# Clearing the padding rows of the first chunk with VectorE and ScalarE, and a reordered prologue, in a fused Fourier-mixing and SwiGLU kernel

## The chip, the cores and the metric

The kernel runs on one core of one Trainium2 chip. The core has a matrix engine (TensorE, PE in the profile; its weight loads are PEld), VectorE (DVE), ScalarE (ACT), GpSimd (POOL) and SyncE (SP), and 16 DMA engines that move data for all of them. The metric is the device time of one launch in microseconds. Before the change it was 624.73 us, the median of five runs (624.17 to 628.4).

## What is computed

The input `x` is 8 x 3008 x 256 (batches, rows, columns) in float32. The kernel takes the real part of the two-dimensional Fourier transform of each batch (over rows and columns) and feeds it, as 24064 tokens of 256 values, to a SwiGLU block with a hidden width of 1536:

```python
def _attn_ref(x):
    X = np.fft.fft(x, axis=1)
    X = np.fft.fft(X, axis=2)
    return X.real.astype(np.float32)

def _moe_ref(x, w_gate, w_val, w_out):
    g = x @ w_gate
    silu = g * (1.0 / (1.0 + np.exp(-g)))
    val = x @ w_val
    return (silu * val @ w_out).astype(np.float32)
```

## The kernel before

**The arithmetic.** The transform over the 256 columns is folded into the weights: `w_gate` and `w_val` are multiplied once by cosine and sine tables (`CD`, `SDt`), which gives `Wp`, `Wq` and `Wm` (`Wq` times -2, 0 for the first row). The transform over the 3008 rows is a product with cosine and sine tables `Tab`, after the eight-fold symmetry of the rows has been used up by sums and differences ("folding"). Each batch is therefore held as two chunks of SBUF partitions: chunk A (`XA`, 128 rows of each eighth) and chunk C (`XC`, the remaining `NCR` = 60 rows). In chunk C 64 partitions belong to each half, of which 60 hold rows of the input, one holds row 0, and the rest is padding that has to be zero.

**The main part.** The results of the row transform, `Pt` and `Qt`, are cut into tiles of 512 (the first ones 480) columns. For each tile and each of the 12 slices of the hidden width, TensorE makes the gate and the value (line 904), ScalarE takes SiLU, VectorE and GpSimd make the products `hp` and `hm`, and TensorE multiplies them with `Wo` (line 1144). GpSimd folds the next batches at the same time (lines 157 to 181), SyncE loads them. The order of all instructions of this part comes from a small planner in the file (`Sched.run`), whose costs and due times don't depend on the prologue.

**The prologue.** Batch 0 takes another way, written out by hand in the order of issue of each engine:

- SP and ACT load chunk A of batch 0 (lines 247 and 249, five transfers) and chunk C of batch 0 into a tile of its own, `XC0` (line 260: `what` 2 are the two 240 KB transfers of the rows that run upwards, `what` 0 and 1 the four of 120 KB that run downwards), and row 0 into partitions 60 and 124 (line 261).
- The padding of `XC0` and later that of `XC` is cleared by DMA from a zero row of `sel` (`zeros`, lines 251 and 264, two transfers each). Line 261 writes partitions that line 251 clears, so it waits for these. Then SP issues the loads of batch 1 into `XC` (lines 140 to 144).
- VectorE makes the phase factors `mM` from `pcol`, GpSimd the products `t1` (line 332), VectorE the angles `rr` and `ra` (336, 340), ScalarE the tables `Tab` (343, 346).
- `place` (line 413) puts the rows in order by a product with the 0/1 matrices `putA` and `putC`: `psA` from `XA`, `psC` from the first half of `XC0` (its upward rows). `sums` (422) adds or subtracts the downward rows. `fold_d` (480, 481) folds chunk A on GpSimd and casts on ScalarE to `EOb`; `halves` (426, 427) casts chunk C to `SBc`.
- TensorE then runs `half_folded` (468) on `EOb`, `half_w` (447) on the first third of the weights, `W0` in the code and `W` in the profile, and `unfolded` (475) on `SBc`. ScalarE takes the weights `Wq` (449) and `od` (612) from PSUM, VectorE adds and subtracts to `Pt` and `Qt` (617), and the main part starts.
- The weights are loaded by GpSimd with a cast to bf16 (`load_w`, line 360): `W0` first, the second third after `fold_d`, and the last third after the first `half_w`.

GpSimd also makes `prod` = `df` times `pcol` or `pcol2` (390), from it the angles `rrd` of the column tables (391, 392, 394), and `putC` (395). `d_tables` (402 to 405) makes `CD` and `SDt` on ScalarE.

Every transfer issued by SP or ACT carries one of eight completion counters in turn. The compiled instruction list makes a queue wait, before it issues a transfer, until the last transfer with the same counter has landed. `zero` is a column of zeros, `P` is 128 and `D` is 256.

Of the kernel before, what the change touches and what calls it, by code (L numbers as in the profile page):

```python
# [12 lines left out]
F32 = mybir.dt.float32  # L13
I32 = mybir.dt.int32
BF16 = mybir.dt.bfloat16
AF = mybir.ActivationFunctionType
Alu = mybir.AluOpType
# [14 lines left out]
def kernel(  # L32
# [84 lines left out]
    def rows_at(b, row, ap):  # L117
        return bass.AP(tensor=x.tensor, offset=(b * M + row) * D, ap=ap)
# [118 lines left out]
    nc.vector.memset(zero, 0.0)  # L237
    nc.vector.memset(sel, 0.0)
    nc.scalar.activation(w0[:, 0, 0:1], zero, AF.Silu)
    zrow = sel.bitcast(F32)[1:2, :]  # L240

    def zeros(X, hi):
        dst = X.rearrange("p a q d -> p (a q d)")[64 * hi + NCR:64 * hi + 64, :]
        return dict(out=dst.rearrange("p (k n) -> p k n", n=P // 2),
                    in_=zrow.unsqueeze(1).to_broadcast([1, (64 - NCR) * dst.shape[1] * 2 // P, P // 2]))

    q.dma_start(out=XA3[:, 0:4, :], in_=up_block(0, 1, P))
    for a, eng in ((3, nc.scalar), (2, q), (1, nc.scalar), (0, q)):
        eng.dma_start(out=XA3[:, 4 + a, :], in_=down_set(0, a, JA, LA, NA))
    for hi in range(2):  # L250
        q.dma_start(**zeros(XC0, hi))

# [6 lines left out]
    for hi, what in ((0, 2), (1, 2), (0, 0), (1, 0), (0, 1), (1, 1)):  # L259
        (q, nc.scalar)[hi if what != 1 else 0].dma_start(**xc0(hi, what))  # L260
    q.dma_start(out=XC0[NCR:64 + NCR + 1:64, 0:2, 1],
                in_=rows_at(0, 0, [[2 * R * D, 2], [R * D, 2], [1, D]]))
    for hi in range(2):
        q.dma_start(**zeros(XC, hi))

# [26 lines left out]
    def col(name, n=1, dt=F32):  # L292
        small[name] = tp.tile([P, n], dt, name=name)
        return small[name]
# [13 lines left out]
    m_cols(0, pcol, LA, JA)  # L308
    vts(mM[:, 0:2], mm_[:, 0:2], scalar1=1.0 / M, scalar2=None, op0=Alu.mult)
    half = col("half")  # L310
    vts(half, pcol, scalar1=64.0, scalar2=-64.0, op0=Alu.is_ge, op1=Alu.mult)
# [7 lines left out]
    nc.vector.memset(halfpi, math.pi / 2.0)  # L319
    vts(putA, putA, scalar1=pcol, scalar2=None, op0=Alu.is_equal)  # L320
    nc.vector.memset(EOf[:, 1, :, P:P + 1], 0.0)
# [54 lines left out]
    def ce_angles(ch):  # L376
        rr, ra = ce_angle[ch]
        angles(rr, kf, ch, ti[ch])
        magnitude(ra, rr)

    def ce_tables(ch):
        rr, ra = ce_angle[ch]
        sine(ch, 0, NCE, rr)
        cosine(ch, 0, NCE, ra)

    ce_angles(0)
    nc.vector.memset(Tab[:, :, :, :, NOO - 1:NOO], 0.0)
    ce_tables(0)
    for i, c_ in enumerate((pcol, pcol2)):
        pts(prod[:, i, :], df, scalar1=c_, scalar2=1.0, op0=Alu.mult, op1=Alu.mult)  # L390
    pts(rad.bitcast(I32), prod, scalar1=1.0 / D, scalar2=1.0, op0=Alu.mult, op1=Alu.mult)
    pts(rrd, rad.bitcast(I32), scalar1=-float(D), scalar2=1.0, op0=Alu.mult, op1=Alu.mult)
    load_w(0)
    ptt(rrd, rrd, prod, op=Alu.add)
    pts(putC, putC, scalar1=pcol, scalar2=1.0, op0=Alu.is_equal, op1=Alu.mult)
    ce_angles(1)
    ce_tables(1)
    nc.vector.memset(sel[0:1, :], 1.0)
# [114 lines left out]
    opposite(0)  # L513
    d_tables()
    for a in (0, 2):
        fold_d(0, a)
    sums(SA, 1, XA, psA)
    start_acc(0)
    half_folded(0, 0)
    psC = place(XC0, putC, 2, ((psO, "o"),))  # L520
    half_folded(0, 2)
    weigh_ce()
    opposite(1)
    for a in (0, 2):
# [5 lines left out]
    for a in (0, 2):  # L530
        half_folded(1, a)
    nc.vector.memset(SDt[:, :, 0:1], 1.0)
    hd = tp.tile([P, 2, 2, 1], F32, name="hd")
# [3 lines left out]
    heads(nc.gpsimd, SC[:, 0, 0, :, 0:1], SC[:, 0, 1, :, 0:1], CEc)  # L537
    sums(SC, 1, XC0, psC)
    halves(SBc, SC, 1)
    for k, (pool, nm) in enumerate(((psV, "v"), (psG, "g"))):  # L540
# [982 lines left out]
```

## Time and profile before

| what | value |
|---|---|
| median of five runs | 624.73 us |
| the profiled execution | 624.73 us, its span 623.0 us (1.73 us lie around the span) |
| granted TensorE clock, mean | 0.993 |
| busy, PE / DVE / ACT / POOL | 604.3 / 577.0 / 527.6 / 471.8 us |
| first matmul of the main part (line 904) | 30.53 us after the span's start |
| first matmul of `psC` (line 413 on `XC0`) | 19.24 us |
| first `half_w` matmul (line 447) | 25.36 us |

Starts are given from the span's start. The profile's chain of work is followed back from the last instruction: at each step it names what released that step. A wait "A <- B: total, times, longest" says that engine and line A stood idle until B. In the timeline a row has the start, the duration, the engine and line, and the tiles; rows of one line are merged. A share of DMA time above 1 means that packets of several queues overlap on an engine.

### The profile page before, as it was taken

The page shows a single profiled execution, that of the slowest core. Times are in us where ns is not written, and L with a number is a line of the kernel's source. Part 1 is how long each engine was busy: PE and PEld are TensorE (multiplying, and loading weights), DVE is VectorE, ACT ScalarE, POOL GpSimd, SP SyncE. Part 2 cuts the span into 40 slices and gives each one's busy share as a digit, 9 for nine tenths or more (in the row PEclk, how much of TensorE's full clock was granted, in tenths as well). Part 3 has the DMA queues.
Part 4 walks back from the last instruction along what each step waited for, and adds up shares of the span by engine and source line. Part 5 has one row for each costly group of instructions (what it writes and reads, how often), then busy time and mean ns, then how long its engine had stood idle before and what let it go on. Part 6 is the DMA issues. An engine that isn't in the chain of part 4 may idle for free.

```text
span 623.0 us, 12518 instructions
## 1 busy us (share of the span) xinstructions
PE 604.3 (97%) x4012; PEld 395.4 (63%) x4073; DVE 577.0 (93%) x1054; ACT 527.6 (85%) x1001; POOL 471.8 (76%) x432
## 2 busy tenths in 40 slices
PE   7799989999999999999999999999999999999997
PEld 5445656666666666666666666666666666666676
DVE  7399959999999999999999999999999999999982
ACT  6387556789898999898898899999998988999994
POOL 8499697999887888987888778877787444446652
PEclk9799999999999999999999999999999999999999
DMA  9672645544523513454135112226121111211112
GB/s 219 99 114 49 153 116 147 162 135 116 152 61 82 149 44 95 134 139 128 55 89 150 53 51 78 62 67 165 45 60 52 45 49 47 61 39 58 59 52 77
DMA packets 51340, 57.74 MB, mean 93 GB/s; under 512 B 8002, under 2 KB 38346, under 8 KB 51274
## 3 DMA queue, kind: packets, MB, share of 16 engines
q1 hardware_dynamic: 47592, 53.69, 31.8%
q0 software_dynamic: 3184, 2.36, 3.1%
q10 hardware_dynamic: 498, 0.89, 0.6%
q8 instruction: 32, 0.52, 0.4%
q14 instruction: 34, 0.28, 0.2%
HBM read 29.39 MB, written 24.65 MB: 87 GB/s over the span
## 4 chain that ended last, share of the span: by engine, by line
PE 86%; DVE 6%; DMA 3%; issue 2%; ACT 1%; SPq 1%; DVEq 0%; ACTq 0%
PE o L1144 36%; PE g L904 23%; PE v L904 19%; DVE es L1027 2%; PE g L1287 2%; PE o L1287 2%; DMA XC<-sel 1%; DVE sv L1088 1%; DMA XA<-in_x_dram 1%; DMA XC<-in_x_dram 1%; PE v L1144 1%; PE o L413 1%; PE g L581 1%; DVE hp L942 0%; PE o L581 0%
## 5 line engine op out<-in xcount | busy, mean ns | idle before, releaser
L1095 POOL TENSOR_TENSOR hm<-sv 128x1024 bf16<-128x1024 f32 (+2 forms) x133 | 247.6, 1862 | 120.0 <-ACT sv L1074 66.1
L1088 DVE SCALAR_TENSOR_TENSOR sv<-es,v 128x512 f32<-128x512 f32 (+2 forms) x266 | 177.7, 669 | 1.7 <-issue 0.6
L1098 DVE TENSOR_TENSOR hp<-sp,v 128x512 bf16<-128x512 f32 (+2 forms) x260 | 174.0, 669 | 3.0 <-ACT sp L1071 2.4
L1144 PE MATMUL o<-Wo,hm 128*128 128x256 bf16 (+1 forms) x1128 | 166.4, 273 | 0.7
L1144 PE MATMUL o<-Wo,hp 128*128 128x256 bf16 (+1 forms) x1104 | 165.6, 273 | 0.4
L1144 PEld LDWEIGHTS <-hp 128*128 128x128 bf16 (+2 forms) x1140 | 112.0, 98 | 63.0 <-issue 4.4
L1144 PEld LDWEIGHTS <-hm 128*128 128x128 bf16 (+2 forms) x1140 | 112.1, 99 | 61.1 <-issue 0.4
L1002 ACT ACTIVATE sp<-g 128x512 f32<-128x512 f32 (+2 forms) x202 | 120.0, 594 | 32.9 <-PE g L904 21.9
L1074 ACT ACTIVATE sv<-g 128x512 f32<-128x512 f32 (+2 forms) x202 | 131.5, 652 | 7.2 <-PE g L904 5.1
L904 PE MATMUL v<-Pt,Wp 128*128 128x512 bf16 (+2 forms) x283 | 106.0, 375 | 2.1 <-DVE hp L1098 0.5
L1027 DVE SCALAR_TENSOR_TENSOR es<-bc,w,v 128x512 f32<-128x512 bf16 (+2 forms) x140 | 101.8, 729 | 6.0 <-DMA bc<-br 4.3
L904 PE MATMUL g<-Pt,Wp 128*128 128x512 bf16 (+2 forms) x284 | 106.4, 375 | 0.1
L904 PE MATMUL g<-Qt,Wq 128*128 128x512 bf16 (+2 forms) x242 | 90.5, 374 | 0.3
L976 ACT ACTIVATE v<-bc,w 128x512 f32<-128x512 bf16 (+2 forms) x126 | 87.0, 691 | 0.4 <-DVE hp L1098 0.3
L904 PE MATMUL g<-Qt,Wm 128*128 128x512 bf16 (+2 forms) x219 | 82.0, 374 | 0.2
L1025 ACT COPY es<-v 128x512 f32<-128x512 f32 (+2 forms) x126 | 73.5, 583 | 3.1 <-PE v L904 2.7
L904 PEld LDWEIGHTS <-Wp 128*128 128x128 bf16 x576 | 56.2, 98 | 30.7 <-issue 4.8
L904 PE MATMUL v<-Qt,Wq 128*128 128x512 bf16 (+2 forms) x162 | 60.7, 375 | 3.1 <-DVE es L1027 2.9
L904 PEld LDWEIGHTS <-Wq 128*128 128x128 bf16 x450 | 44.0, 98 | 21.4 <-issue 1.3
L1150 ACT COPY ev<-o 128x512 f32<-128x512 f32 x89 | 53.3, 599 | 4.1 <-PE o L1144 2.9
L904 PE MATMUL v<-Qt,Wm 128*128 128x512 bf16 (+2 forms) x148 | 55.4, 374 | 0.5 <-DVE hp L942 0.5
L904 PEld LDWEIGHTS <-Wm 128*128 128x128 bf16 x372 | 36.4, 98 | 17.8 <-issue 0.2
(191 smaller groups left out, 707.1 us busy)
## 6 DMA issues: line engine op xcount, KB each, us to landing
out_dram<-ev SPq DMA_DIRECT2D x96, 128.0 KB
XA<-in_x_dram SPq DMA_DIRECT2D x30, 256.0 KB
XA<-in_x_dram SPq DMA_DIRECT2D x112, 64.0 KB
XC<-in_x_dram SPq DMA_DIRECT2D x31, 120.0 KB
XC<-in_x_dram SPq DMA_DIRECT2D x105, 32.0 KB
bc<-br SPq DMA_DIRECT2D x21, 128.0 KB
St<-Fc SPq DMA_DIRECT2D x14, 128.5 KB
out_dram<-ev SPq DMA_DIRECT2D x12, 120.0 KB
```

Of the source, the lines that this page charges most:

```text
L904: nc.tensor.matmul(ps[:, :n], Wt[:, gv, fs], src[:, :n], start=start, stop=stop, skip_group_check=True)
L976: nc.scalar.activation(T_[kv][:, :w], bc[t][:, :w], AF.Copy, scale=w0[:, 1, f:f + 1])
L1002: nc.scalar.activation(T_[ksp][:, :w], T_[kg][:, :w], AF.Silu)
L1025: nc.scalar.copy(T_[kes][:, :w], T_[kv][:, :w])
L1027: nc.vector.scalar_tensor_tensor(T_[kes][:, :w], bc[t][:, :w], w0[:, 1, f:f + 1], T_[kv][:, :w], op0=Alu.mult, op1=Alu.add)
L1074: nc.scalar.activation(sv()[:, f % 2, w - 1::-1, 1], T_[kgm if by_dve else kg][:, :w], AF.Silu)
L1088: nc.vector.scalar_tensor_tensor(sv()[:, f % 2, w - 1::-1, 0], T_[kes][:, :w], 2.0, T_[kv][:, :w], op0=Alu.mult, op1=Alu.subtract)
L1095: nc.gpsimd.tensor_tensor(hts_(t)[1][:, f - 1:f + 1, :w], sv()[:, :, :w, 1], sv()[:, :, :w, 0], op=Alu.mult)
L1098: nc.vector.tensor_tensor(hts_(t)[0][:, f, :wp], T_[ksp][:, :wp], T_[kv][:, :wp], op=Alu.mult)
L1144: nc.tensor.matmul(st["ps"][:n, j, :], hts[t][minus][:, f, c:c + n], Wo[:, f, :], start=(f == 0), stop=(f == nF - 1))
L1150: nc.scalar.copy(ev[:, 0:len(pair), :], st["ps"][:, 0:len(pair), :])
L1287: nc.tensor.matmul(st[q][:, cols], l, r_, start=(i == 0), stop=(i == len(mms) - 1), skip_group_check=True)
```

## The change

The padding of `XC0` is no longer cleared by DMA. VectorE writes zeros over the first half of the whole tile (1024 float32 columns on 128 partitions) and ScalarE over the second half, by a copy of the broadcast zero column; the loads of `XC0` come after these. The padding of `XC` is still cleared by DMA, now from row 61 of the cleared `XC0`, in four transfers of 4 x 8 KB rather than two with 256-byte pieces. `prod` goes from GpSimd to ScalarE, `putC` from GpSimd to VectorE, `putA` stands earlier on VectorE. On GpSimd the last step of `rrd` comes before the load of `W0` rather than after it. On ScalarE the last table passes of batch 0 (`weigh_ce`, `opposite(1)`) come before the first casts of `fold_d`, and `d_tables` after them. One small memset of `SDt` moves behind two sums on VectorE. TensorE's instructions and all of the main part stay in the same order.

```diff
     nc.vector.memset(zero, 0.0)
     nc.vector.memset(sel, 0.0)
+    xf = XC0.rearrange("p a q d -> p (a q d)")
+    nc.vector.memset(xf[:, 0:4 * D], 0.0)
     nc.scalar.activation(w0[:, 0, 0:1], zero, AF.Silu)
-    zrow = sel.bitcast(F32)[1:2, :]
-
-    def zeros(X, hi):
-        dst = X.rearrange("p a q d -> p (a q d)")[64 * hi + NCR:64 * hi + 64, :]
-        return dict(out=dst.rearrange("p (k n) -> p k n", n=P // 2),
-                    in_=zrow.unsqueeze(1).to_broadcast([1, (64 - NCR) * dst.shape[1] * 2 // P, P // 2]))
-
     q.dma_start(out=XA3[:, 0:4, :], in_=up_block(0, 1, P))
     for a, eng in ((3, nc.scalar), (2, q), (1, nc.scalar), (0, q)):
         eng.dma_start(out=XA3[:, 4 + a, :], in_=down_set(0, a, JA, LA, NA))
-    for hi in range(2):
-        q.dma_start(**zeros(XC0, hi))
+    nc.scalar.copy(xf[:, 4 * D:8 * D], zero.to_broadcast([P, 4 * D]))
...
+    X3c = XC.rearrange("p a q d -> p (a q d)")
     for hi in range(2):
-        q.dma_start(**zeros(XC, hi))
+        for k in range(2):
+            q.dma_start(out=X3c[64 * hi + NCR:64 * hi + 64, 8 * D * k:8 * D * (k + 1)],
+                        in_=xf[NCR + 1:NCR + 2, :].unsqueeze(1).to_broadcast([1, 64 - NCR, 8 * D]))
...
     vts(mM[:, 0:2], mm_[:, 0:2], scalar1=1.0 / M, scalar2=None, op0=Alu.mult)
+    vts(putA, putA, scalar1=pcol, scalar2=None, op0=Alu.is_equal)
...
     nc.vector.memset(halfpi, math.pi / 2.0)
-    vts(putA, putA, scalar1=pcol, scalar2=None, op0=Alu.is_equal)
...
+    for i, c_ in enumerate((pcol, pcol2)):
+        nc.scalar.activation(prod[:, i, :], df, AF.Copy, scale=c_)
     ce_angles(0)
     nc.vector.memset(Tab[:, :, :, :, NOO - 1:NOO], 0.0)
     ce_tables(0)
-    for i, c_ in enumerate((pcol, pcol2)):
-        pts(prod[:, i, :], df, scalar1=c_, scalar2=1.0, op0=Alu.mult, op1=Alu.mult)
     pts(rad.bitcast(I32), prod, scalar1=1.0 / D, scalar2=1.0, op0=Alu.mult, op1=Alu.mult)
     pts(rrd, rad.bitcast(I32), scalar1=-float(D), scalar2=1.0, op0=Alu.mult, op1=Alu.mult)
+    ptt(rrd, rrd, prod, op=Alu.add)
     load_w(0)
-    ptt(rrd, rrd, prod, op=Alu.add)
-    pts(putC, putC, scalar1=pcol, scalar2=1.0, op0=Alu.is_equal, op1=Alu.mult)
     ce_angles(1)
+    vts(putC, putC, scalar1=pcol, scalar2=None, op0=Alu.is_equal)
     ce_tables(1)
...
     sums(SA, 0, XA, psA)
     opposite(0)
-    d_tables()
+    weigh_ce()
+    opposite(1)
     for a in (0, 2):
         fold_d(0, a)
+    d_tables()
     sums(SA, 1, XA, psA)
     start_acc(0)
     half_folded(0, 0)
     psC = place(XC0, putC, 2, ((psO, "o"),))
     half_folded(0, 2)
-    weigh_ce()
-    opposite(1)
...
-    nc.vector.memset(SDt[:, :, 0:1], 1.0)
     hd = tp.tile([P, 2, 2, 1], F32, name="hd")
...
     sums(SC, 1, XC0, psC)
+    nc.vector.memset(SDt[:, :, 0:1], 1.0)
     halves(SBc, SC, 1)
```

## The prediction

> **What bounds the kernel now.** I read the page first: TensorE is busy for 97% of the span, so the steady part belongs to it and is not touched. Then I read the chain of work for the first 31 us, where the change lies.
>
> ```profile
> span 623.0 us, 12518 instructions
> PE 604.3 (97%) x4012; PEld 395.4 (63%) x4073; DVE 577.0 (93%) x1054; ACT 527.6 (85%) x1001; POOL 471.8 (76%) x432
> ```
>
> ```profile
> 0.74 5.26 DMA XA<-in_x_dram
> 6.01 0.02 issue
> 6.02 8.54 DMA XC<-sel
> 14.57 0.02 issue
> 14.58 4.41 DMA XC<-in_x_dram
> 19.00 0.24 issue
> 19.24 3.75 PE o L413 x4
> ...
> 30.96 0.36 PE g L904
> ```
>
> Columns: start, us, what. The second clearing transfer of XC0 is issued when the first XA transfer has landed (6.01), takes 8.54 us, and only then can row 0 (line 261) be issued, which lands at 18.99. `psC` starts at 19.24. The waits of the first 35 us say the same from the engines' side, and a table by stage shows what else the gap costs: TensorE stands from 13.93 on, its granted clock is 0.50 from 17.5 on, and the `psC` matmuls run at half speed.
>
> ```profile
> DVE SC L422 <- PE o L413: 7.3, 2, 6.3
> PE o L413 <- DMA XC<-in_x_dram: 5.3, 1, 5.3
> 18.00:20.00 2.00, 0.76 (x1) 0.50 (x2) 0.00 (x0) 0.00 (x0) 0.47 (x3) 0.50 1.12 148
> 22.00:24.00 2.00, 2.00 (x6) 0.68 (x5) 0.98 (x4) 0.25 (x1) 0.20 (x2) 0.50 0.40 25
> ```
>
> (Stage rows: busy time of PE, PEld, DVE, ACT, POOL, then the clock, DMA share, GB/s.) What else is due before the main part is in the timeline; these rows give the limits that come next.
>
> ```profile
> 12.75 3.48 POOL L480 TENSOR_TENSOR EOA<-SA 128x512 f32<-128x512 f32 x3 [0.34 <-DVE SA L422]
> 16.09 1.11 ACT L481 CAST EOb<-EOA 128x512 bf16<-128x512 f32 x2
> 25.36 0.60 PE L447 MATMUL v<-W,CD 128*128 128x256 bf16 x4
> 27.07 0.48 ACT L612 COPY od<-v 128x377 f32<-128x377 f32 x1
> ```
>
> **Chunk C: what goes, and when XC0 is complete.** Both clearing transfers leave SP's queue ahead of the XC0 loads. The first upward load can be issued at 2.7, where the first clearing transfer was (before, SP's XC0 loads began at 7.46). The next one inherits the wait for the first XA transfer (6.01), the two after it waits that ended at 7.44 and 9.42 in the trace of before; with 0.95 us of issue each SP is through them at 10.4 and issues row 0 then, instead of at 14.58. The wait on the clearing has gone. Row 0 took 4.41 us to land; the shortest small transfer I find on the chain is `bc<-br` with 2.37. So XC0 stands at 12.8 to 14.8, unless the 0.98 MB of XC0 hold row 0 up. From 2 to 10 us the core moved 246 to 378 GB/s in the 2 us stages, so XA and XC0 (3.08 MB) at 280 GB/s end near 2.5 + 11 = 13.5. I take 14.8.
>
> **The clears.** VectorE's memset is not in the trace: `sel` (64 words) takes 0.11 us and one word 0.06, which makes 0.87 for 1024; two 512-column sums of 0.69 would be 1.37. It is a plain write, so I take 1.1. ScalarE's copy: 377 columns take 0.476 and 512 take 0.599, so 1024 about 1.07. It ends near 3.3, before the load that waits for it has its counter free (6.01): nothing. The ACT queue's own second load waits for it, 3.24 to 3.4: nothing.
>
> **What stands behind the memset on VectorE.** Everything up to the sums, 1.1 later, and `putC` adds 0.28 (the row of `putA`, 0.281). Before, the first sum of chunk A started at 8.23, the others at 9.93, 11.12 and 11.98, when TensorE delivered. Now the first two run from 9.6 to 11.0, and the third is on time again; with the dear end of the memset it starts 0.13 late and the fourth on time. The first fold on GpSimd needs the second sum: 11.0, against a start of 11.32 before. So the cover is TensorE's `psA`, which runs to 11.94; without it the price is 1.4 us. `putA` is ready before XA lands at 6.01 in either place.
>
> **ScalarE.** The table passes follow VectorE by 1.1 and end at 10.2; `opposite` (0.83), `weigh_ce` (0.92) and `opposite` again end at 12.8, so the first `EOb` cast ends at 13.4 instead of 13.07. The second waits for GpSimd until 13.87 as before. `d_tables` (0.42 + 0.51 + 0.49 + 0.20) then ends at 16.1, and the last two casts run from 16.1 to 17.2: exactly as before. Moving them costs nothing because the folds on GpSimd end at 16.2. `prod` takes two passes of 128 columns, between 0.20 (one column) and 0.42 (256), at about 4.5, in ScalarE's idle time of 3.16 us before the first sine.
>
> **GpSimd and the weights.** It loses `prod` (1.25) and `putC` (0.75) but waits for `mM`: both `t1` products end near 6.2, the small memsets and iotas (1.2) near 7.5, three steps of `rrd` (0.57 + 0.58 + 0.75) near 9.5. The two W0 transfers are issued at 9.5 and 10.4, 1.3 later than 8.22 and 9.14. Of them I know how long they take to land:
>
> ```profile
> DMA to landing us min/median/max: 7.9/8.5/9.0
> XA<-in_moe_w_gate_dram POOLq DMA_DIRECT2D x1, 256.0 KB, 9.1
> XA<-in_moe_w_val_dram POOLq DMA_DIRECT2D x1, 256.0 KB, 10.0
> ```
>
> The first line is the tile W, the others are the second third. Before, W0 was there at 18.1 and was first read at 25.36. Now the value part lands at 10.4 + 9.0 to 10.0, 19.4 to 20.4; from below by the 7.9 of the gate part, 18.3. I take 19.9: this hidden transfer becomes the last wait.
>
> [...]
>
> **The sum.** TensorE: first `half_folded` 13.5 to 14.3 (`EOb` 13.4); `psC` 14.8 to 16.9, at 0.51 per instruction as the last `psA` had (1.02 for two) because the gap is short; `half_folded` 0.65 + 1.3, to 18.85 (its casts are there at 17.2). VectorE's sums of chunk C end at 17.6 and 19.0, with 0.69 each; ScalarE's `halves` (1.24 each pair) end at 18.9 and 20.3. `half_w` starts with W0 at 19.9, ends 0.87 later at 20.8, `Wq` takes 0.59, and `od` starts at 21.45 instead of 27.07: 5.6 us earlier. The first `Pt` and line 904 keep their distance from `od`. The bounds: row 0 and W0 at their early ends give `od` near 20.45 (6.6 earlier, 6.8 with the memset at 0.87), W0 at 20.4 gives 5.1; with the memset at 1.37 and a row 0 at 15.2 it is 4.5 to 4.8.
>
> **Does it reach the end?** From `half_w` on the order on every engine is the same, and what follows waits for engines, not for time: the last third of the weights is issued behind `Wm`, batch 1's loads wait for that third and for TensorE. The one clock-bound input is the second third of the weights, issued behind the folds at 16.2 and 16.9, landing near 25.3 and 26.9; it is read at 32.58 and 35.28, now 27.0 and 29.7. GpSimd folds batch 1 from 45.97 and its XC loads were issued by 33.9: both move. So 5.6 us leave the span: 623.0 - 5.6 = 617.4, plus 1.73 around it is 619.1. The profiled time equals the median, so no correction.
>
> **Rivals.**
> - Row 0 stays late (13%). Against: the row of 246 to 378 GB/s. For it: the DMA share is above 1 until 14 us, and row 0 queues behind all of XC0. Landing at 17.4 puts `psC` 1.84 us before 19.24, still at half clock, since the clock fell 3.5 us after the last matmul: 622.9. At 16 the gain is 4, 620.7.
> - The gain is partly given back later (10%). At 79 to 86 us the chain runs through SP's stores, loads of 0.9 us each and `bc<-br`. Had these a cause that doesn't move, up to half is lost: 621.9. Against it: SP waits there for ScalarE's `ev`, which moves.
> - Slower (7%): W0 is starved. Batch 1's XC loads (20 transfers from 16.7 on) move to about 11.5 and run beside W0 on the DMA engines. The gain is gone when the value part needs over 15 us (10.4 + 15 = 25.4, today's start of `half_w`); at 18.5 us the kernel takes 3.5 us more, 628.2. Against it: the second third landed in 9.1 and 10.0 beside those same loads.
>
> **How the numbers follow.** The forecast has 70%, its own range is 617.9 to 620.2 (gains of 6.8 to 4.5). About 0.5%, 3.1 us, is what a measurement can tell from no change: below 621.6 is faster. Faster: the 70%, plus the mild parts of the first two rivals, 78%. Within 0.5%: the rest of these and a little of the third, 15%. Slower: 7%. The range runs from 617.5, which is the largest gain (6.8) and 0.4 more since single runs lie up to 0.56 below the median, to the late row 0 at 622.9; it leaves out the slower rival and a few per cent on the other side.
>
> **What would show it.** In the profile after: `psC` at 14.5 to 15.5 with a granted clock near 1.0, no wait of it over 1 us; `EOb`'s last cast near 17.2; the first `half_w` at 19 to 20.5, released by W0; the first line-904 matmul near 24.9; the same distances from there to 100 us. I am wrong if `psC` starts after 17, if `half_w` waits for W0 beyond 22, or if line 904 starts 5 us earlier and the span doesn't end so.

## The result and the profile after

The changed kernel takes 621.93 us, the median of 25 runs (618.62 to 626.32), against 625.19 us over 46 runs of the kernel before on the same chip: a ratio of 0.9941 with a 95% interval of 0.9927 to 0.9955. It is faster by 3.3 us. On another chip, beside the experiments from the control on, the ratio was 0.991 (0.9879 to 0.9941). The forecast was 619.1 us, within 617.5 to 622.9. The profiled execution took 621.76 us with a span of 620.0, so the gain of 3.0 us lies in the span. Line numbers are a few lines smaller than before: `place` is line 410, row 0 line 255, the first products of the main part line 901.

The page of the changed kernel, its first lines of busy time:

```profile
span 620.0 us, 12522 instructions
PE 602.3 (97%) x4012; PEld 394.3 (64%) x4073; DVE 578.6 (93%) x1056; ACT 529.1 (85%) x1004; POOL 470.1 (76%) x429
```

The chain of work of the changed kernel from 13 to 28 us (start, us, what):

```profile
13.85 1.10 POOL EOA L477
14.95 1.07 issue
16.02 3.75 PE o L410 x4
...
27.84 0.44 PE g L901 x2
```

The 8.54 us of a clearing transfer and the 4.41 us of row 0 are gone from the chain. `psC` starts at 16.02 instead of 19.24. The chain calls the 1.07 us before it "issue", which means that it names no releaser. The completions recorded in the trace name it: row 0's transfer, issued at 10.66, has its two completion records at 15.24 and 15.82, the last of all that `psC` needs. The four `psC` pairs still take 3.75 us, as before, because the clock is at half again. The table by stage (us of the stretch, busy time of PE, PEld, DVE, ACT, POOL, then clock, DMA share, GB/s) shows both:

```profile
12.00:14.00 2.00, 0.37 (x3) 0.24 (x4) 2.00 (x4) 1.77 (x4) 1.79 (x3) 1.00 1.19 228
14.00:16.00 2.00, 0.45 (x3) 0.07 (x2) 0.97 (x2) 1.97 (x6) 1.89 (x2) 0.69 0.68 124
16.00:18.00 2.00, 1.98 (x3) 0.97 (x4) 0.00 (x0) 0.79 (x2) 1.90 (x5) 0.50 0.34 42
```

TensorE was busy for 0.82 of the 4 us from 12 to 16; its granted clock is 0.50 from 14.78 to 21.60. What else is due before the main part, from the timeline of the changed kernel, and the landing times of the tile W:

```profile
11.48 4.66 POOL L477 TENSOR_TENSOR EOA<-SA 128x512 f32<-128x512 f32 x4 [0.56 <-DVE SA L419]
15.66 1.13 ACT L478 CAST EOb<-EOA 128x512 bf16<-128x512 f32 x2
22.50 0.60 PE L444 MATMUL v<-W,CD 128*128 128x256 bf16 x4
24.21 0.47 ACT L609 COPY od<-v 128x377 f32<-128x377 f32 x1
27.67 0.37 PE L901 MATMUL g<-Pt,Wp 128*128 128x480 bf16 x1
```

```profile
DMA to landing us min/median/max: 4.6/5.0/5.4
```

`half_w` starts at 22.50 (before 25.36), `od` at 24.21 (27.07), the main part at 27.67 (30.53): 2.86 us earlier each. From there the distance stays between 2.86 and 3.1 us to the end. W0 was in SBUF at 15.57, seven microseconds before it was read.

**The same kernel, executed again.** The other chip gave another profile of the very same program, and it looks different in its prologue. Its timeline:

```profile
6.53 2.05 PE L410 MATMUL g<-XA,putA 128*128 128x512 f32 x2 [1.06 <-DMA XA<-in_x_dram]
14.40 1.96 PE L410 MATMUL o<-XC,putC 128*128 128x512 f32 x4
18.13 0.60 PE L444 MATMUL v<-W,CD 128*128 128x256 bf16 x4
19.84 0.48 ACT L609 COPY od<-v 128x377 f32<-128x377 f32 x1
23.30 0.37 PE L901 MATMUL g<-Pt,Wp 128*128 128x480 bf16 x1
```

Here the first pair of `psA` took 2.05 us against 1.10 in the first profile, as at half clock, and the last 1.02 in both, so that TensorE stood for 0.71 us in front of `half_folded` instead of 2.06; row 0 landed at 14.21, `psC` started at 14.40 right behind `half_folded`, at full clock, and the main part at 23.30. The span was 616.2 us. So one program starts its main part at 27.67 or at 23.30, and the forecast's 24.9 lies between.

The other executions spread in the same way. One window at half clock of 3.41 us lowers the mean granted clock over 620 us by 0.0028 (an estimate, 0.5 x 3.41 of 620 us), so the mean clock gives about the number of such windows, wherever in the span they lie. The executions whose clock is known, median span in us (number of executions); they come from three chips, those of before mostly from two, those of the changed kernel from the first and one of these two:

| mean granted clock | half-clock windows | before | changed |
|---|---|---|---|
| 0.996 to 1.0 | 0 or 1 | none | 618.0 (14) |
| 0.993 to 0.995 | 2 | 622.9 (7) | 620.6 (16) |
| 0.990 to 0.992 | 3 | 624.8 (28) | 622.5 (4) |
| 0.986 to 0.989 | 4 or 5 | 627.4 (27) | none |

At an equal count the changed kernel is 2.3 us shorter, and it has one to two half windows fewer, of some 2 us each (on the one chip that has the clock of both kernels, a mean of 0.991 before and 0.996 after).

### The profile page after: what moved, and what is told of

Its sections match the earlier page's. It is cut to its first block, busy times and chain, and to the rows that moved or that the text cites. A ratio compares the mean times of both kernels' runs of the same rounds, so it can differ in the third digit from the quotient of the medians.

```text
span 620.0 us, 12522 instructions
## 1 busy us (share of the span) xinstructions
PE 602.3 (97%) x4012; PEld 394.3 (64%) x4073; DVE 578.6 (93%) x1056; ACT 529.1 (85%) x1004; POOL 470.1 (76%) x429
## 4 chain that ended last, share of the span: by engine, by line
PE 87%; DVE 6%; issue 2%; ACT 2%; SPq 1%; DMA 0%; POOL 0%; DVEq 0%; ACTq 0%
PE o L1141 36%; PE g L901 23%; PE v L901 19%; DVE es L1024 2%; PE g L1284 2%; PE o L1284 2%; DVE sv L1085 1%; PE v L1141 1%; PE o L410 1%; PE g L578 1%; PE o L578 0%; DVE hm L959 0%; SPq L142 0%; DVE hp L939 0%; ACT sv L1071 0%
```

## The experiments

One account is tested throughout, theory 1: `psC`'s start, that is row 0's landing, and the clock that TensorE has then carry the time, and what the start of the main part gains is passed on to the end unless the SyncE queue takes some of it near 80 us. Each expectation names its rival, and says what a second theory holds where it numbers one. All kernels are the changed one but for the diff shown. The table gives all of them beside each other; the ratio is to the kernel before in the same rounds, "main" the first product of the main part in the profile, "rest" the profile's span less "main". row_early, keep_warm, both and clear_only ran on one chip, where the changed kernel itself was not run (the kernel before took 628.54 us there), so they compare with it only through the ratio. All others from the control on ran on another, the last four (warm50, row_warm, row_sto, warm_sto) later than the rest.

| kernel | `psC` start, its four pairs | main | span | rest | ratio, 95% interval |
|---|---|---|---|---|---|
| before | 19.24, 3.75 | 30.53 | 623.0 | 592.5 | 1 |
| changed, first profile | 16.02, 3.75 | 27.67 | 620.0 | 592.3 | 0.9941 (0.9927 to 0.9955) |
| changed, again | 14.40, 1.96 | 23.30 | 616.2 | 592.9 | 0.9910 (0.9879 to 0.9941) |
| reorder_only | 18.75, 3.75 | 30.49 | 625.2 | 594.7 | 0.9996 (0.9974 to 1.0017) |
| clear_only | 15.67, 3.75 | 26.52 | 622.7 | 596.2 | 0.9930 (0.9902 to 0.9958) |
| xc_small | 15.44, 3.75 | 27.09 | 621.0 | 593.9 | 0.9913 (0.9883 to 0.9943) |
| row_early | 14.29, 1.88 | 23.10 | 618.1 | 595.0 | 0.9908 (0.9877 to 0.9938) |
| keep_warm | 16.62, 1.96 | 25.52 | 621.3 | 595.8 | 0.9915 (0.9887 to 0.9944) |
| both | 16.52, 1.94 | 25.40 | 622.2 | 596.8 | 0.9923 (0.9894 to 0.9952) |
| warm50 | 14.29, 1.88 | 23.11 | 619.2 | 596.1 | 0.9926 (0.9903 to 0.9950) |
| row_warm | 14.29, 1.88 | 28.63 | 623.6 | 595.0 | 0.9923 (0.9893 to 0.9954) |
| row_bc | 14.29, 1.88 | 23.11 | 619.5 | 596.4 | 0.9909 (0.9880 to 0.9938) |
| row_sto | 14.29, 1.88 | 23.30 | 619.4 | 596.1 | 0.9902 (0.9880 to 0.9924) |
| warm_sto | 14.30, 1.88 | 23.12 | 616.9 | 593.8 | 0.9898 (0.9868 to 0.9928) |

### Which part of the change carries it

**The changed kernel again**, unchanged, as a control beside the kernels that follow.

> The changed kernel itself, once more, beside the next three on one chip. Theory 1 (the prologue carries the gain, and whatever the first main instruction gains is passed on unless the SyncE queue takes some of it at 75 to 92 us): the profile again shows row 0 completing at 15.2 to 15.9, psC starting within 0.3 us of that at half clock, half_w at 22.0 to 22.8, and a span 2.5 to 3.3 us under that of the kernel before; ratio 0.992 to 0.996. If the loss at 75 to 92 us is a matter of chance in one execution and not of the order of issues, this run's main part shows an offset there other than the first profile's by over 1 us.

The ratio, 0.991, came out beyond the expected 0.992 to 0.996, though its interval reaches into that range. The profile was the other prologue shown above, with a row 0 at 14.21 and a `psC` at full clock: what was expected of the prologue fell, and with it the idea that one profile shows what the kernel does. The main part, on the other hand, took 592.9 us from its first product as against 592.3.

**reorder_only**: the new order with the old clearing transfers.

```diff
-    nc.vector.memset(xf[:, 0:4 * D], 0.0)
...
-    nc.scalar.copy(xf[:, 4 * D:8 * D], zero.to_broadcast([P, 4 * D]))
+    for hi in range(2):
+        q.dma_start(**zeros(XC0, hi))
...
-        for k in range(2):
-            q.dma_start(out=X3c[64 * hi + NCR:64 * hi + 64, 8 * D * k:8 * D * (k + 1)],
-                        in_=xf[NCR + 1:NCR + 2, :].unsqueeze(1).to_broadcast([1, 64 - NCR, 8 * D]))
+        q.dma_start(**zeros(XC, hi))
```

> The new order of the prologue's operations with the old clearing transfers. Theory 1 (the clearing transfers delay the loads behind them; the order alone is worth little): the GpSimd queue issues the zero transfers again, W0 lands 8 to 9 us after its issue, row 0 completes after 18, psC starts 18.0 to 19.3, half_w 24.0 to 25.5, span within 1 us of the kernel before's, ratio 0.998 to 1.002. Rival (ScalarE and VectorE work taken from GpSimd carries it): the first sums and folds are early, half_w is at 22 to 23 and the ratio is 0.993 to 0.996 with the old transfers too.

Two rows of its timeline, then the landing times of W:

```profile
14.52 0.61 SPq L261 DMA_DIRECT2D XC<-in_x_dram  x1
...
18.75 3.75 PE L413 MATMUL o<-XC,putC 128*128 128x512 f32 x4 [5.15 <-DMA XC<-in_x_dram]
```

```profile
DMA to landing us min/median/max: 7.7/8.2/8.8
```

Row 0 is issued at 14.52 again, `psC` waits 5.15 us for it, the main part starts at 30.49 and the ratio is 0.9996 (0.9974 to 1.0017). (The zero transfers are issued by SyncE; the expectation's "GpSimd queue" was a slip.) The reordering alone brings nothing that shows.

**clear_only**: the new clearing in the order of the kernel before. Against the kernel before, its diff is the clearing half of the change:

```diff
+    nc.vector.memset(xf[:, 0:4 * D], 0.0)
...
-    for hi in range(2):
-        q.dma_start(**zeros(XC0, hi))
+    nc.scalar.copy(xf[:, 4 * D:8 * D], zero.to_broadcast([P, 4 * D]))
...
-        q.dma_start(**zeros(XC, hi))
+        for k in range(2):
+            q.dma_start(out=X3c[64 * hi + NCR:64 * hi + 64, 8 * D * k:8 * D * (k + 1)],
+                        in_=xf[NCR + 1:NCR + 2, :].unsqueeze(1).to_broadcast([1, 64 - NCR, 8 * D]))
```

> The kernel before with the new clearing alone; prod and putC stay on GpSimd, d_tables ahead of the casts, W0 ahead of the last step of the angles. Theory 1 (the gain is the clearing's, and the reordering only makes room for it): GpSimd, 1.0 us later from the memset on VectorE and without the 2.0 us that the reordering takes off it, starts its folds near 13 instead of 11.5 and ends them near 17.4; the last EOb cast ends near 18.5 in place of 16.8; psC starts near 16 and runs at half clock to 19.8, behind which most of this is hidden: main part 0 to 1 us later than in the changed kernel, span 620 to 621. Theory 2 (the reordering carries the gain): the span is 622.5 or more.

`psC` started at 15.67, at half clock, and the main part at 26.52, no later than in the changed kernel's first profile. The ratio of 0.993 can't be told from the changed kernel's by its interval. The span of 622.7 is above the 622.5 that was to speak for theory 2; but that excess came after the start, with a "rest" of 596.2 and a window at half clock at 84 us, while reorder_only's ratio leaves the reordering nothing. So theory 1 is kept on the ratios, not on this span. What the reorder does is seen only in the row before `psC`: `half_folded` starts at 14.41 here and at 13.63 in the changed kernel, which matters when row 0 lands before that.

**xc_small**: XC cleared by the old transfers of 256-byte pieces, XC0 by the engines.

```diff
...
-        for k in range(2):
-            q.dma_start(out=X3c[64 * hi + NCR:64 * hi + 64, 8 * D * k:8 * D * (k + 1)],
-                        in_=xf[NCR + 1:NCR + 2, :].unsqueeze(1).to_broadcast([1, 64 - NCR, 8 * D]))
+        q.dma_start(**zeros(XC, hi))
```

> The changed kernel, but the buffer XC is cleared by the old transfers of 256-byte pieces instead of four of 4 rows by 4 KB. Theory 1: these pieces run beside the loads of W0 and of row 0 on the same DMA engines, so W0 lands 7 to 9 us after its issue instead of 4.6 and 5.4, row 0 completes 1 to 3 us later than 15.8, psC starts at 16.5 to 18.5, and the span is 0.5 to 2.5 us over the changed kernel's. Rival (the two transfers that cleared XC0 made the old delay, being ahead of row 0 in its queue; those of XC are issued after row 0 and can't hold it): row 0 and psC within 0.4 us of the changed kernel's, W0 later but still ahead of psC's end, time within 0.3%.

(The four new transfers are of 4 rows by 8 KB; "4 KB" was a slip.) Theory 1 as put here fell: `psC` started at 15.44, W landed 5.0 and 6.1 us after its issue, and the ratio is 0.9913. The long landing of W before (7.9 and 9.0 us) and the late row 0 came with the two transfers that cleared XC0, which stood ahead of row 0, not with those of XC.

### What decides when the main part starts

**row_early**: row 0 is issued behind the two upward loads, ahead of the four downward ones.

```diff
-    for hi, what in ((0, 2), (1, 2), (0, 0), (1, 0), (0, 1), (1, 1)):
-        (q, nc.scalar)[hi if what != 1 else 0].dma_start(**xc0(hi, what))
+    for hi in range(2):
+        (q, nc.scalar)[hi].dma_start(**xc0(hi, 2))
     q.dma_start(out=XC0[NCR:64 + NCR + 1:64, 0:2, 1],
                 in_=rows_at(0, 0, [[2 * R * D, 2], [R * D, 2], [1, D]]))
+    for hi, what in ((0, 0), (1, 0), (0, 1), (1, 1)):
+        (q, nc.scalar)[hi if what != 1 else 0].dma_start(**xc0(hi, what))
```

> The changed kernel with one transfer moved: row 0 (4 KB, line 255) is issued on SP right behind the first upward load of XC0, at about 3.4 us, not behind the downward loads at 10.66. Theory 1 (the last thing psC waits for is row 0, which lands near 16.0 because it stands behind all the other loads): psC starts when the first half_folded ends, 14.4 to 14.8, the gap on TensorE shrinks from 1.6 to under 0.5 us, half_w starts 1.2 us earlier or more (21.3 or less, against 22.5), the span is 618.8 or less on average. Theory 2 (psC waits for the upward loads themselves or for another engine): psC stays at 15.8 to 16.2 and the span at 620.

**keep_warm**: more of the filler products on `sel` that `warm` issues, to keep TensorE busy.

```diff
-    warm(20)
+    warm(50)
...
     half_folded(0, 0)
+    warm(24)
     psC = place(XC0, putC, 2, ((psO, "o"),))
```

> The changed kernel with more filler matmuls on the zero tile: 50 in place of 20 behind psA, and 24 more between the first half_folded and psC. Nothing else moves. Theory 1 (the part of the forecast gain that is missing is the halved clock from 14.7 to 21.7 us): psC still starts at 15.9 to 16.3 but its four instructions take 2.1 us in place of 3.75, the granted clock is 1.0 from 14 to 22 us, half_w starts at 20.0 to 20.6 in place of 22.5, the main part 2 us earlier, and the span is 617.5 to 618.2, with less spread between executions. Theory 2 (ScalarE's casts or the W0 transfer would take over as the limit at once): half_w starts at 21.5 or later and the span falls by less than 1 us.

**both**: the two together.

```diff
+    for hi in range(2):
+        (q, nc.scalar)[hi].dma_start(**xc0(hi, 2))
...
-    warm(20)
+    warm(50)
...
+    warm(24)
```

> Both edits: row 0 early and the filler matmuls (with 24 of them ahead of psC, which end near 16). If the clock is most of the loss this gives the same 617.5 to 618.2 as the filler alone, since the filler itself holds psC to about 16; if row 0 is most of it, it is slower than row 0 early alone by up to 1.5 us. The casts of chunk A end at 16.8 and W0 is there at 15.6, so half_w can't start before about 18.9.

The timelines at `psC`, of row_early, then of keep_warm, then of both:

```profile
14.29 1.88 PE L412 MATMUL o<-XC,putC 128*128 128x512 f32 x4
```

```profile
16.62 1.96 PE L410 MATMUL o<-XC,putC 128*128 128x512 f32 x4 [0.83 <-POOL EOA L477]
```

```profile
15.18 1.50 PE L438 MATMUL o<-sel 128*128 128x128 bf16 x24
16.52 1.94 PE L412 MATMUL o<-XC,putC 128*128 128x512 f32 x4
```

In row_early row 0 was issued at 5.91, not at 3.4 as expected, and landed at 12.03. `psC` follows `half_folded` at once and the main part starts at 23.10, 7.4 us earlier than before. With the filler and a row 0 that landed at 16.42, `psC` ran at full clock though late, and the main part started at 25.52, 2.15 us earlier than in the changed kernel's first profile though row 0 landed 0.6 us later: the half clock cost over 2 us there. In "both" the filler itself stood before `psC` (15.18 to 16.52). So row 0 and the clock each carry a part of the start. That an early row 0 by itself keeps the clock is not shown: row_early has the 2.06 us of idle time in front of `half_folded` as well, but there the clock's windows parted it in two (busy for 50% and 73%). The end did not follow: in keep_warm and both what follows the start is 3.3 and 4.3 us longer than in the kernel before, and the median spans, 619.25 in row_early and 621.35 in keep_warm, are above the expected 618.8 and 618.2; see below.

**warm50**: only the first of the two fillers.

```diff
-    warm(20)
+    warm(50)
```

> The changed kernel with warm(50) for warm(20), and nothing else: TensorE's filler work after the first sums lasts until about 13.5 (or 14.8, where psA ran at half clock) instead of 11.6. Theory 1 (in the changed kernel's first profile psC and half_folded ran at half clock because TensorE had too little work in one of the clock's 3.41 us windows): no window at half clock between 12 and 30 us; psC starts with row 0's completion or the end of the filler work, 14.6 to 15.9, and its four pairs take 1.7 to 2.1 us instead of 3.75; half_w at 18.3 to 19.8; first main instruction 23.5 to 25.0 instead of 27.67. Span 616.3 to 618.6 where 75 to 92 us cost nothing more, to 621.5 where they do; ratio 0.988 to 0.993. Rival (row 0's landing alone decides, the clock is a by-product): first main instruction still after 26.5.

```profile
10.28 2.96 PE L436 MATMUL o<-sel 128*128 128x128 bf16 x50 [0.58 <-DVE sel L395]
...
14.29 1.88 PE L410 MATMUL o<-XC,putC 128*128 128x512 f32 x4
```

In its timeline the filler lasts until 13.24, and no half window follows before 80.57. Row 0 landed at 13.84 in this execution, without having been moved, so `psC` could start even earlier than expected and the main part at 23.11. The span of 619.2 and the ratio of 0.9926 are no better than the changed kernel's.

**row_warm**: row_early with a shorter filler.

```diff
-    warm(20)
+    warm(36)
```

> row_early with warm(36) for warm(20). Theory 1: as in row_early psC follows half_folded at once, 14.3 to 15.0, at full clock in every phase of the clock's windows; half_w 17.9 to 18.6, first main instruction 23.1 to 23.8. The span depends on 75 to 92 us alone: 615.8 to 616.8 without a loss there, 618 to 620 with; ratio 0.987 to 0.992, no better than row_early's 0.9908 by more than 0.003, since row_early's profile was at full clock already. Rival: a shorter start always carries to the end; then the ratio is under 0.987.

`psC` came at 14.29 as expected, the main part at 28.63, which neither side expected. The timeline of VectorE:

```profile
20.29 1.89 DVE L421 TENSOR_TENSOR SC<-o,XC 128x512 f32<-128x512 f32 x3 [4.20 <-DMA XC<-in_x_dram]
```

The sums of chunk C wait for a load of XC0. Two of these loads show 14 completion records by 14.91 and 16.16 and the fifteenth at 17.42 and 20.17 (in row_early all fifteen by 14.23 and 15.72), and W's value part has its last at 19.09. With these late shares the main part started 5.5 us later than in row_early. The first `half_w` stood for 2.75 us until 22.26, behind the memset of `SDt`, which the change had moved behind two of these sums; what this place alone cost is not parted, since `unfolded` waits for the same sums.

### Where an earlier start is lost again

In row_early the waits from 74 to 112 us and the windows of its clock show the place:

```profile
DVE es L1026 <- DMA bc<-br: 6.2, 1, 6.2
PE v L903 <- DVE es L1026: 4.4, 1, 4.4
```

```profile
77.55:80.96 3.41, 0.00 (x0) 0.00 (x0) 0.32 (x1) 0.16 (x1) 3.33 (x5) 1.00 0.40 97
80.96:84.38 3.42, 2.94 (x10) 1.43 (x10) 3.33 (x6) 0.18 (x1) 3.07 (x6) 0.50 0.42 128
```

VectorE waits for `bc`, TensorE has nothing for a whole window, and the next window is at half clock. In the two profiles of the changed kernel the same wait is 4.1 and 4.3 us, TensorE is busy for 47% or more of each window there, and the clock stays. The three next kernels tried to take the wait away.

**row_bc**: row_early, and the load of `bc` for the third tile ahead of four loads of XC. The plan's due time of one operation and the assumed latency of another are changed for that tile alone:

```diff
-                    S.add("SP", 0.55, all_rows(tr + 1), r=[(("br", tr + 1), 0)], w=[(("bc", tr + 1), 0)], new=[("bc", tr + 1)], lat=3.0)
+                    S.add("SP", 0.55, all_rows(tr + 1), r=[(("br", tr + 1), 0)], w=[(("bc", tr + 1), 0)], new=[("bc", tr + 1)], lat=3.0,
+                          shift=-0.01 if tr == 1 else 0.0)
...
-                    S.add("SP", 0.55, first_rows16(tr + 1), r=[(("pq", tr + 1), "Q")], w=[(("br", tr + 1), 0)], new=[("br", tr + 1)], lat=2.6)
+                    S.add("SP", 0.55, first_rows16(tr + 1), r=[(("pq", tr + 1), "Q")], w=[(("br", tr + 1), 0)], new=[("br", tr + 1)],
+                          lat=0.4 if tr == 1 else 2.6)
```

> row_early (row 0's transfer issued right behind the two upward loads), and in the third part of the main loop the load of bc is put ahead of three loads of XC and one small one in SyncE's queue (0.64 us and 2.75 us of issues that stood between the stores and bc). Theory 1 (the gain of an earlier start is lost at 75 to 92 us because bc is issued too late): psC 14.3 to 14.6 at full clock, first main instruction 23.0 to 23.6 as in row_early; bc issued 3.0 to 3.6 us earlier than 77.80; VectorE's wait for bc falls from 6.2 us to under 3.2; the offset against the kernel before stays at 6.4 to 7.4 us after it, span 615.6 to 616.8, ratio 0.985 to 0.990. Rival (the main part has another limit there: the loads of XC that are now behind bc, or the folds themselves): bc is early but the offset still falls to 4.2 to 5, span 617.6 to 618.8, with a wait for XC or for psum in place of that for bc.

Its timeline (VectorE, then GpSimd) and a wait of ScalarE:

```profile
78.74 1.41 DVE L1026 SCALAR_TENSOR_TENSOR es<-bc,w,v 128x512 f32<-128x512 bf16 x2 [4.19 <-DMA bc<-br]
...
93.55 2.35 POOL L157 TENSOR_TENSOR SDf<-XC 128x1020 f32<-128x1020 f32 x1 [6.49 <-DMA XC<-in_x_dram]
```

```profile
ACT sv L1073 <- POOL hm L1094: 3.1, 1, 3.1
```

`bc` is issued at 75.96, 1.8 us earlier than in row_early (3.0 to 3.6 were expected). The wait for `bc` falls from 6.2 to 4.2 us, the clock stays full to the end, and 7.4 us of lead over the kernel before are still there at 85 us. Then the fold of XC on GpSimd, which waits for the loads that now stand behind, starts at 93.55 instead of 91.91, the product `hm` behind it is late, and at 105 us the lead is 4.0. In this execution the rival is right: the wait only changes its owner, and the span of 619.5 is even above the rival's 618.8.

**row_sto**: row_early, with three stores moved behind `bc` in the finished order, so that both `bc` and the loads of XC come earlier.

```diff
+            sp = [o for o in order if o.eng == "SP"]
+            br, bc2 = [[k for k, o in enumerate(sp) if (name, 2) in o.owners and (name, 2) in o.new][0] for name in ("br", "bc")]
+            late = [o for o in sp[br:bc2] if any(w_[0] == "ev" for w_ in o.owners)]
+            order = [o for o in order if o not in late]
+            k = order.index(sp[bc2]) + 1
+            order[k:k] = late
             for o in order:
                 o.fn()
```

> row_early, and in SyncE's queue the three stores of 120, 8 and 96 rows that stand between the load of br and that of bc at 73 us are issued after bc instead: three loads of XC and bc then come 1.3 us earlier, the stores 4.0 us later; no other order changes. Theory 2 (what stands ahead of bc in SyncE's queue eats the gain at 75 to 92 us): bc issued 4.0 to 4.3 us after br instead of 5.5, VectorE's wait for bc 4.0 to 5.2 us instead of 6.2, offset against the kernel before at 95 us -5.4 to -7.0 instead of -4.2, span 615.6 to 617.2; ratio 0.986 to 0.990. Rival (the late stores hold ScalarE's next copies to ev, or the region is bound elsewhere): a wait of ScalarE for a store or of GpSimd for XC over 1.5 us takes the place, span 618 to 620.

**warm_sto**: the same with `warm(36)`.

```diff
-    warm(20)
+    warm(36)
```

> row_sto with warm(36). Theories 1 and 2 together: first main instruction 23.1 to 23.8, offset against the kernel before -6 to -7.3 us from there to the end, no window at half clock between 12 and 75 us; span 615.3 to 617.0, ratio 0.985 to 0.989, the fastest of these kernels. Rival: as for row_sto, span 618 to 620.

SyncE's order is the same in both kernels. Two rows of each timeline, the issue of `bc` and VectorE's wait for it, first row_sto, then warm_sto:

```profile
78.47 0.61 SPq L1428 DMA_DIRECT2D bc<-br  x1
81.37 1.41 DVE L1032 SCALAR_TENSOR_TENSOR es<-bc,w,v 128x512 f32<-128x512 bf16 x2 [7.03 <-DMA bc<-br]
```

```profile
75.28 0.61 SPq L1428 DMA_DIRECT2D bc<-br  x1
78.16 1.41 DVE L1032 SCALAR_TENSOR_TENSOR es<-bc,w,v 128x512 f32<-128x512 bf16 x2 [3.56 <-DMA bc<-br]
```

In both `bc` is issued 4.1 us after `br` (5.5 in row_early), as expected, and their main parts start within 0.2 us of each other; yet `bc` is issued 3.2 us later in row_sto. The queue falls back between 52 and 68 us, where its issues wait for the landing of earlier loads: from the load of the second tile's `br` to that of the third's, SyncE took 27.7 us in row_sto, 24.8 in warm_sto, 26.0 in row_early, 24.2 in the changed kernel's second profile, 24.0 in its first and 24.6 in the kernel before. So theory 2 of these runs, that the order in front of `bc` eats the gain, holds only in part: in these single profiles the pace of the landings decides more. In warm_sto the wait stayed at 3.6 us and no window at half clock occurred, but 1.9 us of its lead went after 96 us.

The column "rest" says it for all: 592.3 to 596.8 us. It is 594.7 in reorder_only, which starts as late as the kernel before, and 592.9 in the execution of the changed kernel that starts at 23.3; among the starts from 23 to 28 us no order is seen. The loss is a cost that some executions pay, early start or late. The clock agrees: 55 of the 62 executions of the kernel before show about three half windows or more, and its profile had two, both of them before the main part; where the others lay, no run shows. Two points at 30 us are too few to exclude that it is a little rarer there. No variant is shown to beat the changed kernel: the interval of each overlaps the control's 0.9879 to 0.9941, that of the lowest ratio, warm_sto's 0.9898, over most of its width.

## Why the prediction was right, and where not

**Bound and place of the gain: right; the size in part by luck.** The gain is in the prologue, `clear_only` and `reorder_only` put it into the clearing transfers, and in the two profiles of the changed kernel 2.86 and 7.23 us at the first product of the main part became 3.0 and 6.8 us at the end. "So 5.6 us leave the span" lies between the two; the medians differ by 3.3. The prediction's own range for its sum was 617.9 to 620.2, and it called only a time below 621.6 faster: 621.93 misses both (though 3.3 us is just over the 3.1 that it set as the least that can be told), and lies inside 617.5 to 622.9 because the upper end was taken from the rival with a late row 0. As a ratio the sum says 0.991 (619.1 / 624.73). The other chip measured just that; on the first the interval, 0.9927 to 0.9955, doesn't reach it. Of the signs named in advance, the first profile shows the last cast of `EOb` and the equal distances up to 100 us; `psC` and its clock, `half_w` and line 904 all came late.

**Row 0 at 14.8: the size varies.** The issue at 10.66 and 10.07 (forecast 10.4) is right. Over the kernels that clear XC0 with the engines and leave row 0 in its place it took 4.0 to 5.4 us and landed between 13.84 and 16.42; the forecast's 14.8 is near the middle, its bounds of 12.8 to 14.8 were too early. It took 4.41 us before and 4.0 in reorder_only, so the clearing held its issue, not its landing. What took these 4 KB 4.0 us and more, while loads of XC0 and W were on their way, no run shows.

**`psC` "at 0.51 per instruction … because the gap is short": this step failed in the first profile, and not through row 0 alone.** The window of the clock from 11.37 to 14.78 decided. TensorE was busy for 1.02 us of it; of the 2.39 us in which it stood, 2.05 lie in front of `half_folded`, which waited for ScalarE's first cast, and only 0.34 in front of `psC` (the other 1.23 us of that wait came later). With row 0 in time this window would still have been busy for only some 40% (an estimate, 1.02 + 0.34 of 3.41 us), and windows of 40 and 41% were followed by half clock in xc_small and clear_only. The prediction put the gap in front of `half_folded` at nothing. It had read from the trace of before that `psA` "runs to 11.94", where most of `psA` ran at half clock (2.05, 1.92 and 1.40 us a pair, the last 1.02); in the first profile the clock was full from 4.54 on, `psA` ended at 9.92 and the filler behind it at 11.58. In the second profile `psA` ended at 11.80, and the reason given held. From `psC`'s start to `half_w` it took 6.48 us (16.02 to 22.50); the forecast had 4.05 (14.8 to 18.85), and at full clock it was 3.73 (14.40 to 18.13). So 1.2 us of row 0 and 2.4 us of clock were missing. A part of this stood in the first rival, which had the half clock for a landing of 17.4; its "At 16 the gain is 4, 620.7" is within 1.1 us of the profiled 621.76.

**W0 as "the last wait" at 19.9: wrong, it was no wait.** W0 landed 4.6 and 5.4 us after its issue, at 15.57, and 4.8 and 7.5 us after it in the second profile, at 17.65, half a microsecond before it was read; the forecast had taken 9.0 to 10.0 from the trace of before. With XC0's clearing transfers what had held W0 was gone as well (reorder_only, which keeps them, has 7.7 and 8.8 us). This hid 1.05 us of the error above (18.85 to 19.9) in the first profile, so that `half_w` came 2.6 us late against the forecast (22.50 for 19.9), and made the second profile 1.8 us better than the forecast (18.13). The two errors have opposite signs: that the forecast of 619.1 lies between the two profiled executions, 621.76 and 618.0, is luck.

**The covers held.** The memset took 0.91 us (1.1), ScalarE's copy 1.05 (1.07), `prod` 0.69 for both halves (0.40 to 0.84), the first sum began at 9.97 (9.6), the first fold at 11.48 (11.0), the last `EOb` casts ended at 16.8 (17.2), W0 was issued at 9.25 and 10.19 (9.5 and 10.4). None of them held up `psC` in the first profile, where row 0 came last; but ScalarE's first cast, which ended at 13.58, set the end of the idle time that cost the clock. In the second profile the casts and row 0 were within 0.1 us of each other: with an early row 0 `psC` starts at 14.29, there it started at 14.40.

**The four transfers that clear XC did not hold W0.** They are issued from 11.30 to 13.30, after both transfers of W0 (9.25 and 10.19), and have their last completion records between 16.96 and 19.03, when W0 had landed (15.57, against 18.12 in the kernel before). With the old pieces (xc_small) W0 took 5.0 and 6.1 us to land, against 4.6 and 5.4.

**The rivals.** "Row 0 stays late" (13%) came in a mild form. "Partly given back" (10%) named the right place, 79 to 86 us, and the right queue, but not the reason: the cost does not follow from the earlier start, since reorder_only, which starts late, pays 2.2 us of it as well. W0 starved (7%) was not seen in the changed kernel; the nearest was row_warm, where the last shares of two loads of XC0 and of W0 landed 2.5 to 4.0 us after the other shares.

What stays open: why a load's landing between 52 and 68 us takes longer in some executions, and what shifts row 0 by 2 us between executions. Neither was tried.

## What to carry to other kernels

When a change removes transfers, do not carry landing times over from the trace of before: here W0 landed 4.6 and 5.4 us after its issue where that trace had 7.9 and 9.0, and it was not the next limit. Nor carry over the ends of TensorE's work without the clock that it had: here the same products ended at 9.92 or 11.80, and the earlier end left the longer gap (2.06 us in front of `half_folded` against 0.71) and the slower start. When a wait of TensorE shrinks to some two microseconds, cost the work behind it at both clocks, since here one program ran the four `psC` pairs in 3.75 us in one execution and in 1.96 in another, and forecast the median between them. Judge such a kernel by many executions and their mean clock; a profile shows only one.

## What the runs showed of the hardware

**The clock follows windows with a fixed length, in an unforeseen phase.** In the trace of the kernel before the record of the granted clock begins at 10.43 and changes at 17.26, 24.09 and 621.42, that is at 10.43 + n x 3.41 with n = 2, 4 and 179; in the first profile of the changed kernel it begins at 4.54 and changes at 14.78, 21.60 and 618.94 (n = 3, 5 and 180). In the second the windows lie at 9.77 + n x 3.41: a pair of `psA` took 1.72 us from 8.37 and 1.02 from 9.92. Laid out in this way up to 110 us, every window of all the profiles shows a clock of 0.50 or 1.00 and none between. The windows around `psC`, first profile, then second (PE's busy time is the second figure):

```profile
11.37:14.78 3.41, 1.02 (x8) 0.34 (x5) 3.41 (x7) 3.15 (x7) 3.09 (x3) 1.00 1.19 225
14.78:18.19 3.41, 2.17 (x3) 1.16 (x4) 0.22 (x2) 2.01 (x5) 3.20 (x8) 0.50 0.42 55
18.19:21.61 3.42, 3.42 (x9) 1.21 (x9) 2.46 (x4) 1.07 (x2) 0.50 (x4) 0.50 0.99 168
```

```profile
9.77:13.18 3.41, 3.15 (x25) 1.77 (x23) 3.41 (x8) 3.38 (x5) 2.74 (x4) 1.00 1.00 238
13.18:16.60 3.42, 2.97 (x11) 1.36 (x12) 2.68 (x5) 3.19 (x8) 3.20 (x4) 1.00 0.73 125
```

In the first, TensorE was busy for 1.02 of 3.41 us (30%) and the next window was at half clock; that window was busy for 2.17 us (64%), which did not bring the clock back, a full one did. In the second, the windows lay so that each from 6.36 to 23 us had 87% (2.97 us) or more. In keep_warm they lay almost as in the first, and the longer filler made the deciding window 88% busy; the clock stayed full:

```profile
11.47:14.88 3.41, 3.02 (x47) 2.59 (x45) 3.41 (x6) 3.16 (x6) 3.20 (x3) 1.00 1.18 225
```

Over all these windows a full one busy for 0 to 45% (1.55 us from 3.68 in "both") was followed by half clock, one busy for 42% or more (1.43 us from 98.74 in row_bc) could keep it, and from 10 us on a half window gave the full clock back when busy for 86% or more (2.94 us from 80.96 in row_early) and not when busy for 74% or less (2.54 us from 14.20 in xc_small).

**A half window goes with about 2 us of this kernel's span.** In the table of spans by mean clock neighbouring rows are 1.9 to 2.6 us apart; a straight line through the single executions gives 1.9 us for each window in the changed kernel and 1.8 in the kernel before. That is a little more than the 1.7 us by which TensorE falls back in 3.41 us at half clock. What the idle time that brings the window about costs by itself is not parted from this.

**With the old clearing the loads of GpSimd landed later.** W's two parts landed 4.2 to 7.5 us after their issue where the engines cleared XC0 (both profiles of the changed kernel, clear_only and xc_small; 8.9 once, in row_warm with its late shares), and 7.7 to 9.0 in the two kernels where transfers of 256-byte pieces cleared it (before and reorder_only). Whether the pieces themselves did this or the loads of XC0, which they push back beside W's, no run separates. The same pieces for XC alone, issued after row 0, made no such difference (5.0 and 6.1 in xc_small).
